# Linear attention into a routed expert layer: float32 key-value sums, a planned engine order, regrouped transfers

## The chip, the cores and the metric

One core of a Trainium2 chip runs the whole program in one launch. The metric is the device time in microseconds (us) of one execution, as a median of several runs. A core has five engines with instruction queues of their own: PE (TensorE, matrix products; the loads of its weights are listed apart as PEld), DVE (VectorE), ACT (ScalarE), POOL (GpSimd) and SP (SyncE, which here only issues DMA transfers). TensorE's clock is granted at one of two levels, 1.2 or 2.4 GHz; a "granted clock" of 1.00 in a row means 2.4 GHz throughout the stretch.

## The reference, cut to what matters

```python
q, k, v: [8 batches, 8 heads, 576, 64]; w_phi: [64, 128]
def phi(x):
    proj = x @ w_phi
    proj = proj - max(abs(proj), axis=-1)
    return concat([exp(proj), exp(-proj)])     # 256 features
kv  = phi(k).T @ v          # per batch and head: [256, 64]
z   = sum(phi(k), over the 576 positions)
att = (phi(q) @ kv) / (phi(q) @ z + 1e-6)      # -> x [4608, 512]
x = (((x @ w1) * (x @ w2)) @ w3) @ w_out       # [4608, 512]
e = argmax(x @ w_gate); g = softmax(x @ w_gate)[e]
out = g * (relu(x @ e_w1[e]) @ e_w2[e])        # 8 experts
```

All inputs and outputs are float32.

## The kernel before, in words

Nearly every product is made of three float16 matmuls: each operand is split into a high part and a low part (the value less the high part), and high*high, high*low and low*high are summed in PSUM.

**First part.** The eight batches go in four units of two. In a unit, `group` (line 469) handles two heads at a time, four groups to a unit, 16 groups in all. Keys and queries are loaded (`load`), split (`split`), transposed by DMA (`trans`) and multiplied by w_phi (`proj`, lines 547 and 548), each in three chunks of 128x384. On the key side, per head and chunk: `k_max` and `k_sub` take off the row maximum, `k_exp` (line 575) makes exp(-x) in float32 and, through `exp16` (lines 554 and 556), exp(x) twice, as float16 and float32; `exp_lo` (line 561) makes the low part of exp(x) on DVE. `k_s1` to `k_s3` find, once all three chunks of a head have their maxima, a power of two that scales exp(-x); `k_c1` (ACT, line 604) and `k_c2` (DVE, line 609) split the scaled exp(-x). Values are scaled to a power of two from the sum of their squares (`v_norm`, `v_sum`, `v_scale`) and split by `v_hi` (ACT, line 532) and `v_lo` (DVE, line 540). `k_b` (line 612) then sums phi(k).T @ [v, 1]: for each of ten pieces of a head and each sign it issues three float16 matmuls of 65 columns (line 626), 60 a head, 1920 for 32 of them (two heads of each of 16 groups, both batches of the unit together). `kv_hi` (line 633) and `kv_lo` (line 638) split the sum for the queries, whose side (`q_max` to `q_x`) ends in the 65-column matmuls of line 702 and in `xn`.

After a unit's four groups, `x_prep` and `moe1` (lines 757 and 793) do the dense products: lines 806 to 808 (128x384) and line 843 (128x260); then the routing, and each token's row goes to `rows_d` in DRAM. The next unit's attention runs beside it. In the background `w34_setup` and `moe_weight` convert the dense weights (lines 214 to 218, 404, 411), and `expert_weight` (line 289) does the 16 expert matrices: one load of 2 MB into the single buffer `wf`, squares, a scale, then eight pieces that are split (lines 321 and 325) and stored to `wscr` in DRAM, 256 KB each, through four buffers `pc`.

**Second part.** `phase_b` (line 1155) runs 40 slots of 128 tokens of one expert (lines 1127 to 1129 and 1146 to 1148) with expert weights read from `wscr` by transfers of 4 MB. It lies under `manual_schedule`, as written.

**What sets the order.** Every step is filed by hand with a due time, `at(t, fn)`, offsets in the table `O`; the sorted list is the order in which the program is written. From it the framework lays out each engine's queue in the first part: it picks, by run times of its own, among instructions that it takes to be ready, the earlier written first. On the chip each engine then follows its queue strictly.

Of the kernel before, what the change touches and what calls it, by code (L numbers as in the profile page):

```python
# [8 lines left out]
F32 = mybir.dt.float32  # L9
# [15 lines left out]
NE = 8  # L25
# [11 lines left out]
    k_s1=2.37, k_s2=3.06, k_s3=3.08, k_c1=3.31, k_c2=3.4, k_b=3.51, kv_hi=5.55, kv_lo=5.74,  # L37
# [23 lines left out]
E23 = float(2 ** 23)  # L61


@with_exitstack
def kernel(
# [23 lines left out]
        [NE, P, 2, 2, 4096], F16, name="wscr")  # L89
# [199 lines left out]
    def expert_weight(e, idx, t0):  # L289
        src = (e_w1, e_w2)[idx][e]  # L290
        nk = (4, 8)[idx]
        st = {}

        def load():
            st["wf"] = pools["prep"].tile([P, 4096], F32, tag="wf", name="wf")
            nc.sync.dma_start(st["wf"].rearrange("p (k f) -> p k f", k=nk),
                              src.rearrange("(k p) f -> p k f", p=P))
            st["cm"] = stat.tile([P, 4], F32, tag="ecm", name="ecm")

        def square(j):  # L300
            sq = pools["mp"].tile([P, 2 * DM], BF16, tag="junk", name="junk")
            A.activation(sq, st["wf"][:, j * 1024:(j + 1) * 1024], AF.Square, accum_out=st["cm"][:, j:j + 1])

        def scale0():
            st["cs"] = stat.tile([P, 1], F32, tag="ecs", name="ecs")
            V.tensor_reduce(st["cs"], st["cm"], axis=AX.X, op=ALU.add)

        def scale1():
            st["pn"] = psum.tile([P, 512], F32, tag="ts", bufs=1, name="pe")
            T.matmul(st["pn"][:, 0:1], lhsT=ones32, rhs=st["cs"], start=True, stop=True)  # L310

        def scale2():
            st["s"], si = pow2_scale(st["pn"][:, 0:1], 1, CE[idx], "es")
            if idx == 0:
                V.tensor_copy(fexp[:, e:e + 1], si)
            else:
                V.tensor_tensor(fexp[:, e:e + 1], fexp[:, e:e + 1], si, op=ALU.mult)

        def piece_hi(j):
            st["pc", j] = pools["prep"].tile([P, 2, 512], F16, tag="pc", bufs=4, name="pc")  # L320
# [9 lines left out]
        for j in range(4):  # L330
            at(t0 + O["e_sq"] + O["e_sq_j"] * j, square, j)
# [14 lines left out]
    def w34_setup(t0, dt, t1):  # L346
# [4 lines left out]
        def start():  # L351
            st["wo"] = pools["prep"].tile([P, 8, DM], F32, tag="wf", name="wo")
            wg = su.tile([P, 4, NE], F32, name="wg")
            nc.sync.dma_start(wg, w_gate.rearrange("(k p) e -> p k e", p=P))
            st["wg"] = wg
            st["wog"] = su.tile([P, 8, NE], F32, name="wog")
            for i in range(3):
                f = pools["prep"].tile([P, 2, 512], F16, tag="pc", bufs=4, name="f34")
                st["f34", i] = f.rearrange("p a c -> p (a c)").bitcast(F32)
            st["fg"] = const.tile([P, 8, NE], F32, name="fg")  # L360
# [108 lines left out]
    def group(ui, g, T0):  # L469
# [33 lines left out]
        def v_load(h):  # L503
            vf = att.tile([P, 10, D], F32, tag="vf", bufs=2, name="vf")
            G.memset(vf[64:128, 4, :], 0.0)
            G.memset(vf[0:64, 9, :], 0.0)
            for bb, b in enumerate(bs):
                nc.sync.dma_start(vf[:, 5 * bb:5 * bb + 4, :],
                                  v[b, h0 + h, 0:512, :].rearrange("(p r) d -> p r d", r=4))
                nc.sync.dma_start(vf[64 * bb:64 * bb + 64, 9 if bb else 4, :], v[b, h0 + h, 512:S, :])  # L510
            st["vf", h] = vf

        def v_norm(h):
            vs = att.tile([P, 10, 2, D + 1], F16, tag="vs", bufs=2, name="vs")
            st["ssv", h] = stat.tile([P, 1], F32, tag="ssv", name="ssv")
            A.activation(vs[:, :, 0, 0:D], st["vf", h], AF.Square, accum_out=st["ssv", h])
            st["vs", h] = vs
# [11 lines left out]

        def v_hi(h):  # L530
            vs = st["vs", h]
            A.activation(vs[:, :, 0, 0:D], st["vf", h], AF.Copy, scale=st["sv", h][:, 0:1])
            G.memset(vs[:, :, 0, D:D + 1], ZS)
            G.memset(vs[:, :, 1, D:D + 1], 0.0)
            G.memset(vs[64:128, 4, 0, D:D + 1], 0.0)
            G.memset(vs[0:64, 9, 0, D:D + 1], 0.0)

        def v_lo(h):
            vs = st["vs", h]
            V.scalar_tensor_tensor(vs[:, :, 1, 0:D], st["vf", h], st["sv", h][:, 0:1], vs[:, :, 0, 0:D],  # L540
                                   op0=ALU.mult, op1=ALU.subtract)
# [60 lines left out]
        def k_c1(h, c):  # L602
            hl = att.tile([P, 2, 3, P], F16, tag="k2", bufs=2, name="k2")
            A.activation(hl[:, 0], st["ke2", h, c], AF.Copy, scale=st["fk"][:, h:h + 1])
            st["k2", h, c] = hl

        def k_c2(h, c):
            hl = st["k2", h, c]
            V.scalar_tensor_tensor(hl[:, 1], st["ke2", h, c], st["fk"][:, h:h + 1], hl[:, 0],
                                   op0=ALU.mult, op1=ALU.subtract)  # L610

        def k_b(h, c):
# [4 lines left out]
            kv, vs = st["kv"], st["vs", h]  # L617
            for t in range(3):
                tt = 3 * c + t
                for bb, p0, _ in tile_parts(tt):  # L620
                    tv = 9 if p0 else tt
                    end = tt == 8 or (tt == 4 and bb == 0)
                    for z in range(2):
                        hl = st["k2", h, c] if z else st["k1", h, c][0]
                        for a, b in ((0, 0), (0, 1), (1, 0)):
                            T.matmul(kv[:, bb, z, :], lhsT=hl[:, a, t, :], rhs=vs[:, tv, b, :],
                                     start=False, stop=bool(end and a), skip_group_check=True)

        def kv_hi(h):
            if h == 0:  # L630
                st["kvs"] = att.tile([P, 2, 2, 2, 2, D + 1], F16, tag="kvs", bufs=1, name="kvs")
            for z in range(2):
                A.activation(st["kvs"][:, 0, h, z], st["kv"][:, :, z, :], AF.Copy, scale=2.0 ** -10 if z else 1.0)

        def kv_lo(h):
            ks = st["kvs"]
            for z in range(2):
                V.scalar_tensor_tensor(ks[:, 1, h, z], st["kv"][:, :, z, :], 2.0 ** -10 if z else 1.0, ks[:, 0, h, z],
                                       op0=ALU.mult, op1=ALU.subtract)
# [366 lines left out]
    def load_w(ln, e, cond=None):  # L1006
        kw = dict(cond=cond, cond_hint=False) if cond is not None else {}
        src = wscr[e] if isinstance(e, int) else wscr[bass.ds(e, 1)].rearrange("o p a b f -> (o p) a b f")
        nc.sync.dma_start(wb[ln], src, **kw)

    def open_b():
        right.close()
        pools["wb"] = tc_pool(wb_st, "wb", "right")
        wb[0] = pools["wb"].tile([P, 2, 2, 4096], F16, name="wb0")
        wb[2] = pools["wb"].tile([P, 2, 2, 4096], F16, name="wb2")
# [100 lines left out]
    def slot_l1(n):  # L1116
# [3 lines left out]
        for mh in range(2):  # L1120
            ph = psum.tile([P, 4, P], F32, tag="mm", bufs=3, name="ph")
            for mm in range(4):
                m = 4 * mh + mm
                for kk in range(4):
                    wh = w[:, 0, 0, kk * FF + m * P:kk * FF + (m + 1) * P]
                    wl = w[:, 0, 1, kk * FF + m * P:kk * FF + (m + 1) * P]
# [9 lines left out]
    def slot_l2(n, hT):  # L1136
# [6 lines left out]
        for i2 in range(8):  # L1143
            wh = w[:, 1, 0, i2 * DM:(i2 + 1) * DM]
            wl = w[:, 1, 1, i2 * DM:(i2 + 1) * DM]
# [9 lines left out]
    def phase_b():  # L1155
# [4 lines left out]
        wb[1] = B2["pb"].tile([P, 2, 2, 4096], F16, name="wb1")  # L1160
# [4 lines left out]
        V.tensor_copy(wb[1][:, 0, 0, 0:1], xq[1][:, 0, 0, 0:1])  # L1165
# [29 lines left out]
    at(t_end + 1, phase_bm)  # L1195

# [33 lines left out]
```

## Time and profile before

| | us |
|---|---|
| median of 3 runs | 1639.8 (1636.98 to 1642.35) |
| profiled execution | 1653.94 |
| its span, first to last instruction | 1652.2 |
| mean granted clock of TensorE over the span | 0.936 |
| PE busy | 1428.4 (86%) |
| DVE busy | 1001.4 (61%) |
| ACT busy | 881.7 (53%) |

Busy times count instructions between start and end; ends of matmuls are modelled, and consecutive ones overlap, so a busy PE may have room, and the pace of matmuls is read from their starts. "Idle" before a group is time in which its engine waited just before it, and "<-" names what ended that wait.

### The profile page before, as it was taken

Reading aid. Unit: us, or ns where it says so; the run is one execution under the profiler, and the core shown is the slowest. Engines: PE = TensorE matmul, PEld = TensorE weight load, DVE = VectorE, ACT = ScalarE, POOL = GpSimd, SP = SyncE. Lnnn points to the kernel's source line nnn. Section 1 sums busy time; section 2 is a strip of 40 time slices with the busy share of each in tenths; the row PEclk is TensorE's granted clock in tenths of the full one; section 3 lists DMA queues with packets and bytes.
Section 4 is the critical chain, followed back from the end, with each engine's and each line's share of the span. In section 5 each row is a group of like instructions: output and inputs, shape, how many; then the busy total and the mean of one; then the engine's idle time right before and its main releaser. Section 6 shows DMA issues by size and latency. Waiting matters only on the chain. (4 is left out here: it accounts for less than half of the span.)

```text
span 1652.2 us, 38216 instructions
## 1 busy us (share of the span) xinstructions
PE 1428.4 (86%) x14850; PEld 1032.2 (62%) x14854; DVE 1001.4 (61%) x3031; ACT 881.7 (53%) x1979; POOL 226.9 (14%) x491
## 2 busy tenths in 40 slices
PE   5988877888898796889697998968949999999998
PEld 4665555666665474657475766636746777777775
DVE  6998899987898696879697898434411111111111
ACT  4786688777786685768576777335201111111111
POOL 3313100010111010100101000100102111121110
PEclk9988777998999798999898999979979999999999
DMA  7845245575767775574955665963346346747351
GB/s 200 237 125 157 73 124 100 153 124 126 134 170 124 123 166 66 159 146 115 149 159 97 161 101 139 188 191 116 51 145 193 76 83 172 250 104 178 78 170 31
DMA packets 273043, 225.16 MB, mean 136 GB/s; under 512 B 187221, under 2 KB 244825, under 8 KB 271706
## 3 DMA queue, kind: packets, MB, share of 16 engines
q1 hardware_dynamic: 265306, 202.71, 53.5%
q0 software_dynamic: 7552, 19.97, 4.2%
q8 instruction: 118, 1.93, 0.6%
q14 instruction: 67, 0.55, 0.2%
HBM read 261.22 MB, written 53.67 MB: 191 GB/s over the span
## 5 line engine op out<-in xcount | busy, mean ns | idle before, releaser
L806 PE MATMUL pab<-xT,w 128*128 128x384 f16 x768 | 258.8, 337 | 26.1 <-ACT asb L813 16.1
L1132 DVE SCALAR_TENSOR_TENSOR hT<-ph,hT 128x512 f16<-128x512 f32 x80 | 55.3, 692 | 362.6 <-ACT hT L1131 362.6
L807 PE MATMUL pab<-xT,w 128*128 128x384 f16 x768 | 258.8, 337 | 0.0
L808 PE MATMUL pab<-xT,w 128*128 128x384 f16 x768 | 258.3, 336 | 0.0
L1127 PE MATMUL ph<-xTb,wb 128*128 128x128 f16 x1280 | 218.4, 220 | 22.6 <-DMA xTb<-rw 22.6
L843 PE MATMUL py<-w,gt 128*128 128x260 f16 (+1 forms) x1728 | 213.6, 278 | 16.5 <-ACT yb L850 12.1
L1128 PE MATMUL ph<-xTb,wb 128*128 128x128 f16 x1280 | 218.3, 220 | 0.0
L1129 PE MATMUL ph<-xTb,wb 128*128 128x128 f16 x1280 | 218.3, 220 | 0.0
L843 PEld LDWEIGHTS <-gt 128*128 128x128 f16 x1728 | 166.6, 100 | 43.3 <-issue 13.3
L1131 ACT ACTIVATE hT<-ph 128x512 f16<-128x512 f32 x80 | 47.8, 597 | 187.5 <-PE ph L1129 187.5
L1127 PEld LDWEIGHTS <-wb 128*128 128x128 f16 x1280 | 125.9, 98 | 27.9 <-DMA xTb<-rw 21.1
L1128 PEld LDWEIGHTS <-wb 128*128 128x128 f16 x1280 | 125.9, 98 | 4.5
L1129 PEld LDWEIGHTS <-wb 128*128 128x128 f16 x1280 | 125.9, 98 | 0.0
L1150 ACT ACTIVATE ob<-pob,scb 128x512 f32<-128x512 f32 x40 | 27.5, 687 | 183.4 <-PE pob L1148 183.4
L554 ACT ACTIVATE q<-pjT,nM 128x384 f16<-128x384 f32 x192 | 114.9, 598 | 17.2 <-PE nm L702 14.1
L702 PE MATMUL nm<-kvs,q 128*128 128x65 f16 (+1 forms) x1920 | 86.7, 201 | 41.3 <-DVE nx L712 37.4
L1146 PE MATMUL pob<-wb,hT 128*128 128x512 f16 x320 | 121.3, 379 | 0.0
L1147 PE MATMUL pob<-wb,hT 128*128 128x512 f16 x320 | 121.3, 379 | 0.0
L1148 PE MATMUL pob<-wb,hT 128*128 128x512 f16 x320 | 121.3, 379 | 0.0
L321 ACT ACTIVATE pc<-wf,ess 128x512 f16<-128x512 f32 x128 | 88.8, 726 | 57.2 <-DMA wscr<-pc 50.1
L556 ACT ACTIVATE e<-pjT,nM 128x384 f32<-128x384 f32 x192 | 116.0, 604 | 5.8 <-DVE q L561 5.8
L702 PEld LDWEIGHTS <-q 128*128 128x128 f16 (+1 forms) x1920 | 76.9, 104 | 66.1 <-issue 38.0
(255 smaller groups left out, 3237.5 us busy)
## 6 DMA issues: line engine op xcount, KB each, us to landing
wb<-wscr SPq DMA_DIRECT2D x40, 4096.0 KB
wf<-in_moe_w_dram SPq DMA_DIRECT2D x16, 2048.0 KB
wscr<-pc SPq DMA_DIRECT2D x128, 256.0 KB
raw<-in_moe_w_dram SPq DMA_DIRECT2D x32, 512.0 KB
rows_d<-row SPq DMA_DIRECT2D x32, 256.5 KB
kf<-in_k_dram SPq DMA_DIRECT2D x64, 128.0 KB
vf<-in_v_dram SPq DMA_DIRECT2D x64, 128.0 KB
qf<-in_q_dram SPq DMA_DIRECT2D x64, 128.0 KB
```

Of the source, the lines that this page charges most:

```text
L556: A.activation(e1, src, AF.Exp, scale=sgn * ES, bias=bias)
L702: T.matmul(nm[p0:p1, t, z, :], lhsT=hl[:, a, t, p0:p1], rhs=st["kvs"][:, b, h, z, bb, :], start=(a == b), stop=bool(a), skip_group_check=True)
L806: T.matmul(ps, lhsT=wh, rhs=xT[:, 0, kk], start=(kk == 0), stop=False)
L807: T.matmul(ps, lhsT=wh, rhs=xT[:, 1, kk], start=False, stop=False)
L808: T.matmul(ps, lhsT=wl, rhs=xT[:, 0, kk], start=False, stop=(kk == 3))
L843: T.matmul(py, lhsT=gT[i][:, a, t * P:(t + 1) * P], rhs=w34[:, i, b, hf, 0:cw], start=(i == 0 and a == b), stop=bool(i == 7 and a))
L1127: T.matmul(ph[:, mm, :], lhsT=wh, rhs=xT[:, 0, kk, :], start=(kk == 0), stop=False)
L1128: T.matmul(ph[:, mm, :], lhsT=wh, rhs=xT[:, 1, kk, :], start=False, stop=False)
L1129: T.matmul(ph[:, mm, :], lhsT=wl, rhs=xT[:, 0, kk, :], start=False, stop=(kk == 3))
L1146: T.matmul(po, lhsT=hT[:, 0, i2, :], rhs=wh, start=(i2 == 0), stop=False)
L1147: T.matmul(po, lhsT=hT[:, 0, i2, :], rhs=wl, start=False, stop=False)
L1148: T.matmul(po, lhsT=hT[:, 1, i2, :], rhs=wh, start=False, stop=(i2 == 7))
```

## The change

Three things are edited in the first part; the second part's arithmetic is unchanged.

1. `k_b` multiplies float32 exponentials with float32 values, one matmul in place of three. exp(x) and exp(-x) are made once each; the splits of both and of v go. The scales that these splits carried are applied in `kv_hi` and `kv_lo`, for the 64 sums and for the count column apart, with three small DVE instructions a head (`kv_s`) to make them. The count column of ones lies in `vf`, whose rows are 65 wide now.
2. Just before the second part is written, `plan` reads all instructions written so far, gives each a duration (in the diff in ns: `hold`, for which it occupies its engine, and `time`, until its result is there), simulates the engines with their dependencies and buffers (each engine takes, among those ready, the earliest written) and chains each engine's instructions in the resulting order.
3. Transfers: the two heads' loads of keys or queries become one transfer; each 2 MB load of expert weights becomes four of 512 KB, due 0.4 apart; the 128 stores of split pieces become 64 of 512 KB (two pieces in one of two buffers). `wscr` is laid out so that such a store is one run of 4 KB in a partition; the second part indexes it accordingly.

```diff
+class Step:
...
+        if self.dma:
+            if self.engine == "Pool":
+                self.hold, self.time = 1250, 10000
+            elif kind == "DmaTransposeAnt":
+                self.hold, self.queue, self.time = 1300, 1250, 2000
+            else:
+                self.hold, self.queue, self.time = 480, 100 + b / 280, 2000
+        elif kind == "Matmult":
+            n *= 4 if inns[0].dtype == F32 else 1
+            self.hold = max(28, n / 2.4 + 2) * 1.0
+            self.time = self.hold + 170
...
+        else:
+            if self.engine == "DVE":
+                t = 145 + n * (1.1 if two or psum or kind == "TensorReduce" else 0.6)
+            elif self.engine == "Pool":
+                t = 150 + n * (2.2 if two else 1.2)
+            else:
+                t = 200 + 0.93 * n
...
+            self.hold, self.time = max(62, t - OVERLAP[self.engine]), t
...
+def plan(tc, insts, follows):
...
+    for _ in steps:
+        t, e = min((max(free[e], 0.0 if takes[e] else waits[e][0][0]), e) for e in engines if takes[e] or waits[e])
+        while waits[e] and waits[e][0][0] <= t:
+            heapq.heappush(takes[e], heapq.heappop(waits[e])[1])
+        n = heapq.heappop(takes[e])
...
+        if e in prev:
+            tc.add_manual_dep(s.ins, prev[e].ins.name, info, reason="planned order")
+        prev[e] = s
...
-            nc.sync.dma_start(st["wf"].rearrange("p (k f) -> p k f", k=nk),
-                              src.rearrange("(k p) f -> p k f", p=P))
+        def load_part(j):
+            k0, kn = j * nk // 4, nk // 4
+            nc.sync.dma_start(st["wf"].rearrange("p (k f) -> p k f", k=nk)[:, k0:k0 + kn, :],
+                              src[k0 * P:(k0 + kn) * P, :].rearrange("(k p) f -> p k f", p=P))
...
-            nc.sync.dma_start(wscr[e, :, idx, :, j * 512:(j + 1) * 512], pc)
+            if j % 2:
+                nc.sync.dma_start(wscr[e, :, idx, j - 1:j + 1], st["pp", j // 2])
...
-                for h in range(2):
-                    nc.sync.dma_start(
-                        t[:, h, 5 * bb:5 * bb + 4, :],
-                        src[b, h0 + h, 0:512, :].rearrange("(p r) d -> p r d", r=4))
+                nc.sync.dma_start(
+                    t[:, :, 5 * bb:5 * bb + 4, :].rearrange("p h r d -> p h (r d)"),
+                    src[b, h0:h0 + 2, 0:512, :].rearrange("h (p r) d -> p h (r d)", r=4))
...
-            vf = att.tile([P, 10, D], F32, tag="vf", bufs=2, name="vf")
+            vf = att.tile([P, 10, D + 1], F32, tag="vf", bufs=2, name="vf")
+            G.memset(vf[:, :, D:D + 1], 1.0)
...
         def k_exp(h, c):
-            e2 = att.tile([P, 3, P], F32, tag="ke2", bufs=3, name="ke2")
-            A.activation(e2, pm, AF.Exp, scale=-ES)
-            exp16(("k1", h, c), pm, 1.0, "k1", 3)
-            st["ke2", h, c] = e2
+            for z in range(2):
+                e = att.tile([P, 3, P], F32, tag="ke%d" % (z + 1), bufs=3, name="ke%d" % (z + 1))
+                A.activation(e, pm, AF.Exp, scale=-ES if z else ES)
+                st["ke", z, h, c] = e
...
                     for z in range(2):
-                        hl = st["k2", h, c] if z else st["k1", h, c][0]
-                        for a, b in ((0, 0), (0, 1), (1, 0)):
-                            T.matmul(kv[:, bb, z, :], lhsT=hl[:, a, t, :], rhs=vs[:, tv, b, :],
-                                     start=False, stop=bool(end and a), skip_group_check=True)
+                        T.matmul(kv[:, bb, z, :], lhsT=st["ke", z, h, c][:, t, :], rhs=vf[:, tv, :],
+                                 start=False, stop=bool(end), skip_group_check=True)
...
+        def kv_s(h):
+            ks = stat.tile([P, 3], F32, tag="kss", bufs=3, name="kss")
+            fk, sv = st["fk"][:, h:h + 1], st["sv", h]
+            V.tensor_scalar(ks[:, 0:1], fk, 2.0 ** -10, None, op0=ALU.mult)
+            V.tensor_tensor(ks[:, 1:2], ks[:, 0:1], sv, op=ALU.mult)
+            V.tensor_scalar(ks[:, 2:3], fk, ZS * 2.0 ** -10, None, op0=ALU.mult)
...
+                for (c0, c1), sc in zip(((0, D), (D, D + 1)), st["kss", h][z]):
+                    A.activation(st["kvs"][:, 0, h, z, :, c0:c1], st["kv"][:, :, z, c0:c1], AF.Copy, scale=sc)
...
-            for fn in (v_load, v_norm, v_sum, v_scale, v_hi, v_lo, k_s1, k_s2, k_s3, kv_hi, kv_lo):
+            for fn in (v_load, v_norm, v_sum, v_scale, k_s1, k_s2, k_s3, kv_s, kv_hi, kv_lo):
...
-                for fn in (k_max, k_sub, k_exp, k_c1, k_c2, k_b):
+                for fn in (k_max, k_sub, k_exp, k_b):
-                at(tk + O["k_lo"], exp_lo, ("k1", h, c))
...
+    def plan_a():
+        body = max(nc.cur_f.blocks, key=lambda b: len(b.instructions))
+        plan(tc, list(body.instructions), (("su", "mp"), ("att", "wb"), ("att", "tb")))
+    at(t_end + 0.99, plan_a)
```

## Rows read from the trace of the kernel before

**Rows 1.** The chain that ended last, first piece: start us, us, what.

```profile
1627.97 0.98 DMA out_dram<-ob,ix
```

**Rows 2.** Windows by stage: us, busy PE, PEld, DVE, ACT, POOL, PEclk, DMA, GB/s.

```profile
0.00:36.00 36.00, 18.82 (x91) 17.18 (x91) 19.93 (x46) 14.09 (x28) 10.96 (x48) 1.00 0.74 202
36.00:1030.00 994.00, 837.06 (x8855) 602.98 (x8860) 845.20 (x2605) 727.55 (x1695) 120.95 (x343) 0.91 0.62 135
1030.00:1220.00 190.00, 148.57 (x1106) 101.85 (x1104) 78.11 (x262) 64.84 (x138) 18.14 (x22) 0.91 0.56 128
1220.00:1652.00 432.00, 423.92 (x4800) 310.18 (x4800) 58.18 (x121) 75.25 (x120) 76.88 (x78) 0.99 0.51 138
```

**Rows 3.** The same view in stretches of 50 us, four of the attention stage.

```profile
400.00:450.00 50.00, 45.61 (x534) 34.91 (x532) 42.97 (x143) 39.81 (x94) 7.18 (x23) 1.00 0.63 138
...
500.00:550.00 50.00, 36.13 (x303) 23.67 (x302) 36.32 (x123) 26.60 (x66) 4.45 (x13) 0.83 0.84 114
...
600.00:650.00 50.00, 34.17 (x368) 23.50 (x365) 31.99 (x115) 28.72 (x68) 6.96 (x19) 0.86 0.74 102
650.00:700.00 50.00, 45.76 (x531) 34.94 (x530) 43.60 (x139) 38.78 (x92) 4.66 (x20) 1.00 0.56 157
```

**Rows 4.** Waits: who <- for whom: us in total, times, longest.

```profile
ACT pc L321 <- DMA wscr<-pc: 50.1, 13, 17.9
...
ACT junk L302 <- DMA wf<-in_moe_w_dram: 35.9, 10, 11.8
...
DVE sp L491 <- DMA qf<-in_q_dram: 23.3, 4, 16.6
PE ph L1127 <- DMA xTb<-rw: 22.6, 2, 20.9
```

**Rows 5.** Groups by form: DVE instructions that the change removes.

```profile
L609 DVE SCALAR_TENSOR_TENSOR k<-ke,fk,k 128x384 f16<-128x384 f32 x96 | 59.7, 623 | 1.7 <-ACT k L604 1.7
...
L561 DVE TENSOR_TENSOR k<-e,k 128x384 f16<-128x384 f32 x96 | 54.0, 562 | 22.9 <-ACT e L556 20.6 <-ACT k L554 2.0
...
L540 DVE SCALAR_TENSOR_TENSOR vs<-vf,vss,vs 128x640 f16<-128x640 f32 x32 | 28.6, 892 | 0.3 <-ACT vs L532 0.2
```

**Rows 6.** Groups by form: ACT instructions that the change removes.

```profile
L604 ACT ACTIVATE k<-ke,fk 128x384 f16<-128x384 f32 x96 | 56.4, 607 | 18.5 <-DVE fk L599 9.6 <-PE kv L626 8.2 <-DVE w L274 0.6
...
L554 ACT ACTIVATE k<-pm 128x384 f16<-128x384 f32 x96 | 50.1, 522 | 5.3 <-PE kv L626 5.3
...
L532 ACT ACTIVATE vs<-vf,vss 128x640 f16<-128x640 f32 x32 | 26.8, 838 | 2.7 <-DVE vss L194 2.3 <-DVE vsi L196 0.4
```

**Rows 7.** Groups by form: small instructions on DVE and ACT.

```profile
L721 DVE TENSOR_TENSOR rec<-rec,svi 128x6 f32<-128x6 f32 x48 | 7.6, 158 | 0.1
...
L586 ACT ACTIVATE rk<-mk 128x9 f32<-128x9 f32 x32 | 6.9, 216 | 4.7 <-DVE mk L566 4.7
```

**Rows 8.** Timeline of PE, three stretches: start us, us to the last end, instruction, count.

```profile
63.35 1.85 PE L411 MATMUL pg<-wog,w3t 128*128 128x8 f32 x16
65.06 0.27 PE L615 MATMUL kv<-zero 128*128 128x260 f16 x1
...
71.98 1.88 PE L404 MATMUL p<-wo,w3t 128*128 128x512 f32 x4
73.69 0.60 PE L396 MATMUL pt<-ident,w 128*128 128x128 f32 x4
...
680.22 0.90 PE L626 MATMUL kv<-vs,k 128*128 128x65 f16 x24
680.96 0.27 PE L843 MATMUL py<-w,gt 128*128 128x260 f16 x1
```

**Rows 9.** DMA queue of SP: packets, MB, share of 16 engines; two issue groups.

```profile
q1 hardware_dynamic: 265306, 202.71, 53.5%
...
wf<-in_moe_w_dram SPq DMA_DIRECT2D x16, 2048.0 KB
...
vf<-in_v_dram SPq DMA_DIRECT2D x64, 128.0 KB
```

More of the change, by code (lines that the diff above doesn't have):

```diff
@@ L1 @@
+import heapq
+from collections import defaultdict
 from contextlib import ExitStack
@@ L36 @@
     k_load=-4.63, k_split=-2.6, k_trans=-2.5, k_proj=0.05, k_max=0.3, k_sub=0.41, k_exp=0.52, k_lo=0.75,
-    k_s1=2.37, k_s2=3.06, k_s3=3.08, k_c1=3.31, k_c2=3.4, k_b=3.51, kv_hi=5.55, kv_lo=5.74,
+    k_s1=2.37, k_s2=3.06, k_s3=3.08, k_c1=3.31, k_c2=3.4, k_b=3.51, kv_s=3.2, kv_hi=5.55, kv_lo=5.74,
     v_load=-0.7, v_norm=0.3, v_sum=1.05, v_scale=1.55, v_hi=1.7, v_lo=2.54,
@@ L61, with sizes, __init__, cells @@
 E23 = float(2 ** 23)
+BYTES = {F32: 4, I32: 4, F16: 2, BF16: 2, U8: 1}
+OVERLAP = dict(DVE=80, Activation=105, Pool=-25)
+WAKE = 60
+LANES = 8
+SPARE = 0
+DMA_SPARE = 0
+def sizes(ap):
+    n, span = 1, 1
+    for step, count in ap.ap[1:]:
+        n *= count
+        span += (count - 1) * abs(step)
+    return n, span
+class Step:
+    def __init__(self, ins):
+        self.ins, self.engine = ins, str(ins.engine).rsplit(".", 1)[-1]
+        kind = type(ins).__name__.removeprefix("Inst")
+        self.dma = "DMA" in kind.upper()
+        outs = [a for a in ins.outs if hasattr(a, "bass_ap")]
+        inns = [a for a in ins.ins if hasattr(a, "bass_ap")]
+        self.reads, self.writes = [self.cells(a) for a in inns], [self.cells(a) for a in outs]
+        n = max(sizes(a)[0] for a in (outs if kind != "TensorReduce" else inns)) if outs else 1
+        psum = any(c[0] == "P" for c in self.reads)
+        two = sum(sizes(a)[0] > 1 for a in inns) > 1
+        self.queue = 0.0
+        if self.dma:
+            b = n * 128 * BYTES.get(outs[0].dtype, 4)
+            if self.engine == "Pool":
[8 more added lines that the diff above has]
+            self.time = self.hold + 170
+            self.spare = SPARE if sizes(outs[0])[0] < 20 else 0
+        else:
[5 more added lines that the diff above has]
+                t = 200 + 0.93 * n
+            if len(outs) > 1:
+                t += 190
+            self.hold, self.time = max(62, t - OVERLAP[self.engine]), t
+        self.after, self.begins, self.left, self.ready, self.start = [], [], 0, 0.0, 0.0
+    @staticmethod
+    def cells(a):
+        ap = a.bass_ap
+        t = ap.tensor
+        where = str(getattr(t, "space", "DRAM")).rsplit(".", 1)[-1][0]
+        if not hasattr(t, "tag"):
+            return ("D", t.name, None, ())
+        if where != "S":
+            return (where, t.name, t, (0,))
+        b = BYTES.get(a.dtype, 4)
+        row = t.bytes() // 128
+        lo = ap.offset * b % row
+        p0 = ap.offset * b // row
+        hi = lo + sizes(a)[1] * b
+        halves = [h for h, on in ((0, p0 < 64), (1, p0 + ap.ap[0][1] > 64)) if on]
+        return ("S", t.name, t, tuple((k, h) for k in range(lo // 32, (hi - 1) // 32 + 1) for h in halves))
@@ new lines, in plan, with arm @@
+def plan(tc, insts, follows):
+    steps = [Step(i) for i in insts if i.outs and "PoolBoundary" not in type(i).__name__]
+    last, readers, users, uses_pool = {}, defaultdict(list), defaultdict(list), defaultdict(list)
+    order = defaultdict(list)
+    for n, s in enumerate(steps):
+        for _, name, t, _ in s.reads + s.writes:
+            if t is not None:
+                if not users[name]:
+                    order[t.tag].append((name, t.tag_meta.bufs))
+                    pool = t.tag.rsplit("_", 2)[1]
+                    uses_pool[pool].append(name)
+                if users[name][-1:] != [n]:
+                    users[name].append(n)
+    deps, begun = [set() for _ in steps], [set() for _ in steps]
+    for n, s in enumerate(steps):
+        for acc, wr in ((s.reads, False), (s.writes, True)):
+            for w, name, t, cells in acc:
+                for c in cells:
+                    k = (name, c)
+                    if k in last:
+                        deps[n].add(last[k])
+                    if wr:
+                        deps[n].update(readers[k])
+                    elif w == "P":
+                        for m in readers[k][-1:]:
+                            (begun if steps[m].engine == s.engine else deps)[n].add(m)
+        for w, name, t, cells in s.reads:
+            for c in cells:
+                readers[name, c].append(n)
+        for w, name, t, cells in s.writes:
+            for c in cells:
+                last[name, c], readers[name, c] = n, []
+    for n, s in enumerate(steps):
+        if s.dma and s.engine == "SP":
+            for d in [d for d in deps[n] if steps[d].dma and steps[d].engine == "SP"
+                      and {w[1] for w in steps[d].writes} & {w[1] for w in s.writes}]:
+                deps[n].discard(d)
+                begun[n].add(d)
+    for tag, tiles in order.items():
+        for j, (name, bufs) in enumerate(tiles):
+            if j:
+                for n in users[name]:
+                    begun[n].add(users[tiles[j - 1][0]][0])
+            if j >= bufs:
+                old = users[tiles[j - bufs][0]]
+                for n in users[name]:
+                    deps[n].update(old)
+    for a, b in follows:
+        old = [n for name in uses_pool[a] for n in users[name]]
+        for name in uses_pool[b]:
+            for n in users[name]:
+                deps[n].update(old)
+    for n, s in enumerate(steps):
+        deps[n].discard(n)
+        begun[n].discard(n)
+        s.left = len(deps[n]) + len(begun[n])
+        for d in deps[n]:
+            steps[d].after.append(n)
+        for d in begun[n]:
+            steps[d].begins.append(n)
+    free, waits, takes = defaultdict(float), defaultdict(list), defaultdict(list)
+    lanes, queue = [0.0] * LANES, 0.0
+    for n, s in enumerate(steps):
+        if not s.left:
+            heapq.heappush(waits[s.engine], (0.0, n))
+    engines = sorted({s.engine for s in steps})
+    prev = {}
+    info = mybir.DependencyInfo(mybir.DependencyClass.NoSync, mybir.DependencyReason.DATA)
+    def arm(m, r):
+        o = steps[m]
+        o.ready = max(o.ready, r)
+        o.left -= 1
+        if not o.left:
+            heapq.heappush(waits[o.engine], (o.ready, m))
+    for _ in steps:
[3 more added lines that the diff above has]
+        n = heapq.heappop(takes[e])
+        s = steps[n]
+        if s.dma and e == "SP":
+            t = max(t, lanes[0])
+            queue = max(queue, t + s.hold) + s.queue
+            end = queue + s.time
+            lanes = lanes[1:] + [end]
+        else:
+            end = t + s.time
+        s.start, free[e] = t, t + s.hold
+        for m in s.after:
+            o = steps[m]
+            if o.engine != e or s.dma:
+                arm(m, end + WAKE + (o.spare if o.engine == "PE" else 0) + (DMA_SPARE if s.dma and o.engine != "SP" else 0))
+            else:
+                arm(m, t if e == "PE" else end + 35)
+        for m in s.begins:
+            arm(m, t)
+        if e in prev:
+            tc.add_manual_dep(s.ins, prev[e].ins.name, info, reason="planned order")
+        prev[e] = s
+    return steps
@@ L528, in v_scale @@
             st["sv", h] = s
[L530 to L541, printed above, removed]
         def proj(nm, h, c):
@@ L637, in kv_lo @@
             for z in range(2):
-                V.scalar_tensor_tensor(ks[:, 1, h, z], st["kv"][:, :, z, :], 2.0 ** -10 if z else 1.0, ks[:, 0, h, z],
-                                       op0=ALU.mult, op1=ALU.subtract)
+                for (c0, c1), sc in zip(((0, D), (D, D + 1)), st["kss", h][z]):
+                    V.scalar_tensor_tensor(ks[:, 1, h, z, :, c0:c1], st["kv"][:, :, z, c0:c1], sc,
+                                           ks[:, 0, h, z, :, c0:c1], op0=ALU.mult, op1=ALU.subtract)
         def q_max(c, h):
```

52 lines of the change are left out of this document (24 added, 28 removed).

## The prediction

> **What bounds the kernel now.** The chain of waits comes first and helps little: it starts at 1628 us [rows 1] and holds only the last outputs. So I read the windows by stage, then the same view finer, then the waits. The stages [rows 2] are a start of 36 us; the attention stage to 1030, with dense products and conversions beside it; a tail of 190, the last unit's dense products; and the second part, 432, where PE is busy for 424 and which the change only indexes differently. The attention stage has no single bound. Of its 994 us PE is busy 837, DVE 845, ACT 728, and TensorE's clock is granted at 0.91 of 2.4 GHz. The finer windows [rows 3] show two kinds. In some, the clock is 1.00 and PE is busy 45.6 or 45.8 of 50, with DVE at 43 to 44. In others PE and DVE both drop to 32 to 36, with the DMA share up to 0.84. The waits [rows 4] say that transfers are part of these dips: ACT waits 50.1 us for stores of expert pieces and 35.9 for the 2 MB loads, DVE 23.3 for query loads, once for 16.6. PE, DVE and ACT lie close together, so taking work off one of them is worth little unless the order fills the others.
>
> The profiled execution took 1653.9 us, 1.7 outside its span. The median of the runs is 1639.8, so I make the sum on the profiled execution and multiply by 1639.8/1653.9 = 0.9915.
>
> **Part 1, float32 sums.**
> DVE loses three groups [rows 5]: 59.7 + 54.0 + 28.6 = 142.3 us. It gains 64 one-column instructions in kv_lo and 3 x 32 in kv_s, 160 at the 158 ns of a 128x6 instruction [rows 7], 25 us. Net -117.
> ACT loses 56.4 + 50.1 + 26.8 = 133.3 us [rows 6] and gains 64 small instructions in kv_hi at 216 ns [rows 7], 14 us. Net -119.
> PE: before, 24 matmuls of line 626 take 0.74 us from the first start to the next group's start [rows 8], 31 ns each; 1920 take 59 us. After, there are 640 float32 matmuls of 65 columns. The trace has no such shape. A float32 matmul in the code leaves two records, and there are two neighbours [rows 8]. At 8 columns, 16 records take 1.71 us, 107 ns each. At 512 columns, 4 records take 1.71 us, 428 ns each, so columns cost 0.84 ns and 65 would cost 54. Since 8 columns can't fill 107 ns, that is the weight load, and it hides under long column streams but not under 54 ns. Lower end: only columns, 2 x 54 = 108 ns, 69 us. Upper end: load and columns in turn, 2 x 161 = 322 ns, 206 us. I take 2 x 107 = 214 ns, 137 us, nearest to the 8-column row. Net +78, from +10 to +147. The planner itself prices such a matmul at 260/2.4 + 2 = 110 ns, so it fills about 66 us of PE time twice over.
> Beside this, the Trainium skill, "FP8 and Floating Point Precision", section "TensorE Precision Notes", counts true FP32 as four passes through the array. The 512-column row agrees, but by passes alone 65 columns come to an estimated 108 ns and the sum to +10 instead of +78; the 8-column row stands against that.
> Waits: k_b now needs only k_exp and the values, no longer the scale found from all three chunks, so a chain of ACT, PE and DVE leaves its path. In exchange vf is held until the head's last k_b where it was free after v_lo. Behind a late vf stand, on SP's queue, the key loads and transposes, and DVE and PE wait for those. There are two buffers and v_load is due 2.8 steps of the due times (9 make a group) after the k_b that frees its buffer, so I charge nothing.
>
> **Part 3, transfers.** A 2 MB load no longer keeps the queue for itself; this can return part of the 35.9 and 23.3. Pieces are stored in pairs through two buffers, so ACT may wait longer for each; I leave the 50.1 between 0 and 100 at its value. SP issues 64 fewer key and query loads, 64 fewer stores, 48 more expert loads. Against it, a row of vf of 65 values cuts the 64 large value loads [rows 9] from 1 KB runs to 256 B, 512 for 128 packets each: 24,600 more. At the queue's mean, 53.5% of 1652 us x 16 over 265,306 packets = 53 ns, that is 82 us on each of 16 engines, against as many packets fewer in the stores, whose bytes remain. Bounds: nothing, and 0.08 more of DMA share in 994 us. Cover is the prefetch of values; I charge nothing and keep it in the range.
>
> **Part 2, the order, and the sum.** PE becomes the busiest engine of the attention stage: 837 at 0.91 clock is 762 at full clock, plus 78 is 840. DVE comes to 728, ACT to 609. What counts is how full PE is, times its clock, over the stage: now 762/994 = 0.77. With 840 the stage breaks even at 0.845. The windows without dips reach 0.91 at clock 1.00 [rows 3], with DVE at 0.87, more than it will then need (728/920 = 0.79). I expect the plan with less DVE and ACT work to hold that mean: 840/0.913 = 920, -74 us. In the tail, 190 less 149 busy is 41 idle, of which 21 is the wait for the first rows of the second part [rows 4], which no edit touches; I take half of the other 20, -10. The start and the second part: 0. Sum -84: 1653.9 - 84 = 1570, times 0.9915 = **1557 us**.
>
> **Rivals.**
> *PE binds at its present fill* (slower). The added 78 us sit on an engine that stalls as before, since plan and chip differ by 104 ns on each of 640 matmuls and a fixed order can't give way. At 0.77, 840/0.77 = 1091, +97: 1736. For it: the dips are transfers' and the bytes stay. Against: DVE and ACT, for which PE waits, lose 14% and 16%. It decides below 0.845. Chance 0.12.
> *The order gives nothing* (no change). The framework already fills the queues by times of its own; only the trade remains, PE lands at about 0.845, and 1640 stays. For it: windows at 0.91 exist already. Against: they alternate with windows at 0.68 to 0.72. Chance 0.11.
> *DVE stays the bound* (faster still). If PE's extra work all falls into its 157 idle us, the stage goes with DVE at its present fill: 728/0.85 = 856, -138, with the tail -148: 1493. For it: with 845 of 994 us it is the busiest of the three now, and what it loses is the largest single saving. Against: PE would have to be 840/856 = 0.98 full. Chance 0.12.
>
> **How the numbers follow.** The forecast has 0.65, within itself 1505 to 1610 (fill 0.96 to 0.88 with the same tail: 840/0.96 = 875 gives 1512; 840/0.88 = 955 gives 1591; the rest is the price of the float32 matmul). The range 1490 to 1640 takes in the DVE case, the no-change case and both ends of PE's price at the forecast's fill (+10 gives 1483, +147 gives 1632, nearly all of it inside), and leaves out the slow rival and a little below. A measurement of this kernel can tell about 0.3% from no change. Faster by more: the forecast, the DVE case and half of no change, 0.82; same 0.04; slower 0.14.
>
> **What would show it.** Right: L561 for k, L609, L540, L604 and L532 gone; twice 640 float32 records at 107 ns start to start; the attention stage near 920 us with PE above 0.9 in most 50 us windows, clock near 1.00, DVE near 0.8; waits for wf and qf shorter; tail and second part within 10 us. Wrong: float32 records at 54 or 161 ns; dips with high DMA share that remain; PE waiting on DMA for Tkf, or SP on PE for vf; PE fill times clock under 0.845.

## The result and the profile after

The change takes 1614.4 us (1611.4 to 1618.0) against 1640.4 for the kernel before: ratio 0.984, interval 0.981 to 0.987; in a later comparison 0.986 (0.982 to 0.990). It is faster, by 26 us where 83 were forecast. The profiled executions differ by 36 us in span (1652.2 and 1616.1); the one of before lay 0.9% over its median, the one after 0.2%, so some 10 of these 36 us belong to the two executions and not to the change.

The page of the kernel after, part 1, engine TensorE:

```profile
PE 1488.6 (92%) x14212; PEld 1125.3 (70%) x14214; DVE 908.2 (56%) x2967; ACT 789.1 (49%) x1819; POOL 201.5 (12%) x395
```

PE is 60 us busier and DVE and ACT are each 93 us less busy. The windows by stage, after (columns as in [rows 2], which they answer):

```profile
0.00:36.00 36.00, 23.08 (x113) 21.74 (x113) 18.09 (x36) 13.52 (x26) 11.70 (x44) 1.00 0.82 236
36.00:1000.00 964.00, 893.45 (x8195) 691.34 (x8197) 755.17 (x2565) 636.21 (x1539) 97.45 (x252) 0.94 0.66 137
1000.00:1190.00 190.00, 153.66 (x1170) 107.53 (x1169) 76.96 (x247) 64.69 (x136) 15.33 (x21) 0.91 0.55 135
1190.00:1616.00 426.00, 418.44 (x4741) 304.71 (x4738) 57.97 (x120) 74.66 (x119) 77.05 (x78) 1.00 0.52 137
```

The attention stage went from 994 to 964 us, where 920 were forecast. The tail's windows are 190 us wide by choice of their ends; its length is read from single lines below. PE's work in the stage, 893 at a clock of 0.94, is 840 us at full clock, the forecast's 840 (within some 4 us, as the clock has two digits). What is short is how full the stage is: 840/964 = 0.87, not 0.91.

Cut at the first unit's end, before and after (windows, same columns; before first):

```profile
36.00:260.00 224.00, 183.99 (x1723) 129.33 (x1727) 201.99 (x550) 170.94 (x392) 46.01 (x100) 0.84 0.52 140
260.00:1000.00 740.00, 627.15 (x6849) 453.08 (x6849) 618.78 (x1977) 535.30 (x1250) 73.89 (x240) 0.94 0.65 133
```

```profile
36.00:260.00 224.00, 201.29 (x1577) 154.23 (x1578) 179.35 (x545) 146.76 (x350) 35.97 (x74) 0.87 0.53 135
260.00:1000.00 740.00, 692.15 (x6620) 537.11 (x6620) 575.82 (x2022) 489.45 (x1190) 61.48 (x178) 0.96 0.69 138
```

After, PE busy times clock is 0.78 of the first unit and 0.90 of the rest. The first unit's end and the start of the second part are read from the first start of lines 806 and 1127, by the view of single lines (instruction, count, least/median/greatest ns, first and last start); the end of the whole attention stage is read from the last start of line 702, the queries' last products. Before:

```profile
L702 PE MATMUL nm<-kvs,q x1920: 190/194/263, 76.1 to 1022.9; 128*128 128x65 f16 x160, 128*64 128x65 f16 x32
...
L806 PE MATMUL pab<-xT,w x768: 322/326/528, 265.1 to 1181.6; 128*128 128x384 f16 x192
...
L1127 PE MATMUL ph<-xTb,wb x1280: 216/219/314, 1220.9 to 1641.1; 128*128 128x128 f16 x183
```

After, the same three lines of the program:

```profile
L878 PE MATMUL nm<-kvs,q x1920: 190/194/263, 77.1 to 991.7; 128*128 128x65 f16 x160, 128*64 128x65 f16 x32
...
L981 PE MATMUL pab<-xT,w x768: 322/326/528, 263.3 to 1144.9; 128*128 128x384 f16 x192
...
L1303 PE MATMUL ph<-xTb,wb x1280: 216/219/314, 1184.5 to 1604.9; 128*128 128x128 f16 x183
```

The first unit ends 2 us sooner and the attention stage 31; from there to the second part it is 193 us in place of 198, so the tail is 5 us shorter. The second part begins 36 us sooner and then takes as long as before. So nearly the whole gain lies in the units after the first.

### The profile page after: what moved, and what is told of

Same layout as the page of the kernel before. It is cut to its first block, busy times and chain, and to the rows that moved or that the text cites. A ratio compares the mean times of both kernels' runs of the same rounds, so it can differ in the third digit from the quotient of the medians.

```text
span 1616.1 us, 36510 instructions
## 1 busy us (share of the span) xinstructions
PE 1488.6 (92%) x14212; PEld 1125.3 (70%) x14214; DVE 908.2 (56%) x2967; ACT 789.1 (49%) x1819; POOL 201.5 (12%) x395
## 5 line engine op out<-in xcount | busy, mean ns | idle before, releaser
L1018 PE MATMUL py<-w,gt 128*128 128x260 f16 (+1 forms) x1728 | 206.0, 274 | 0.0
L791 PEld LDWEIGHTS kv<-vf,ke 128*128 128x128 f32 x1280 | 172.9, 211 | 12.2 <-issue 7.4
L791 PE MATMUL kv<-vf,ke 128*128 128x65 f32 x1280 | 176.3, 291 | 3.8 <-issue 2.1
L738 DVE TENSOR_TENSOR q<-e,q 128x384 f16<-128x384 f32 x192 | 108.0, 565 | 36.9 <-ACT e L733 35.8
L982 PEld LDWEIGHTS <-w 128*128 128x128 f16 x768 | 78.4, 102 | 57.5 <-issue 19.4
```

Source lines behind the costliest of these rows:

```text
L791: T.matmul(kv[:, bb, z, :], lhsT=st["ke", z, h, c][:, t, :], rhs=vf[:, tv, :], start=False, stop=bool(end), skip_group_check=True)
L982: T.matmul(ps, lhsT=wh, rhs=xT[:, 1, kk], start=False, stop=False)
L1018: T.matmul(py, lhsT=gT[i][:, a, t * P:(t + 1) * P], rhs=w34[:, i, b, hf, 0:cw], start=(i == 0 and a == b), stop=bool(i == 7 and a))
```

## The experiments

All ratios are to the kernel before on the same chip, with 95% intervals.

### Which part of the change brings the gain

The three parts of the diff were applied in other combinations: the order alone, the sums alone, the sums with the transfers, the order with the transfers, and the order with the sums. In each the hunks of the other parts are left out, so their lines are those of the kernel before.

```diff
 (order alone; order with the float32 sums, old transfers; order with new transfers, float16 sums)
+    at(t_end + 0.99, plan_a)
 (sums alone; sums with new transfers)
...
+                        T.matmul(kv[:, bb, z, :], lhsT=st["ke", z, h, c][:, t, :], rhs=vf[:, tv, :],
+                                 start=False, stop=bool(end), skip_group_check=True)
```

Expected of the order alone:

> Only the planned order is added; float16 sums and old transfers stay. Theory A (PE is the bound of the attention stage, the order raises its fill, the float32 sums put 78 us of weight loading back on it): most of the gain is here, 1590 to 1620, PE at 0.85 or more of the stage with DVE near 0.9. Theory B (the framework's order was as good; the gain came from the DVE and ACT work removed): 1640 within 5. Theory C (the plan's prices do not hold and its fixed order loses): above 1650.

Of the sums alone:

> Only the float32 sums; the framework's order and old transfers stay. Theory A: PE gets 78 us more in a stage that it fills to 0.84, DVE and ACT lose 117 and 119: between 1630 and 1680. Theory B: 1615, all of the gain. Theory C: below 1615.

Of the sums with the transfers:

> The change without the planned order. Theory A: 1630 to 1670, so the order is worth 20 to 55 us on top of the other two. Theory B: 1615, the order is worth nothing. Theory C: below 1610, the order costs.

Of the order with the transfers:

> The change without the float32 sums: planned order and new transfers with the three float16 matmuls. Theory A: the float32 sums are what keeps the stage long, so this is faster than the whole change, 1570 to 1605. Theory B: 1640. If DVE becomes the bound instead (845 us of work in the stage), the same as the whole change, 1610 to 1620.

Of the order with the sums:

> Planned order and float32 sums with the old transfers. If the regrouped transfers are worth what the waits of the kernel before suggest: 5 to 15 us slower than the whole change, ratio 0.988 to 0.994. If the planned order had already gone around them, or the smaller runs of the values cost it back: 0.982 to 0.988.

Of the change itself, beside later kernels:

> The changed kernel itself, beside the next three and the kernel before on one chip: ratio to before 0.984 as in the first comparison, which places the runs of the planned order with float16 sums (0.988) within 0.005 of it.

| order | sums | transfers | ratio | interval |
|---|---|---|---|---|
| framework | float32 | old | 0.998 | 0.996 to 1.001 |
| framework | float32 | new | 0.9995 | 0.997 to 1.002 |
| planned | float16 | old | 0.990 | 0.987 to 0.993 |
| planned | float16 | new | 0.988 | 0.983 to 0.993 |
| planned | float32 | old | 0.993 | 0.991 to 0.996 |
| planned | float32 | new | 0.984, 0.986 | 0.981 to 0.990 |

The gain is the order's: 1.0% alone, about 1.5% on top of the other two. It isn't one lucky order, for every planned kernel here and below that does the whole arithmetic lies at 0.968 to 0.993. Theory B falls: without the order, sums and transfers are worth nothing measurable. Theory A is right on the order and wrong on the sums: they neither keep the stage long nor shorten it, with or without the order. The order with float16 sums came out as the whole change does, as was expected if DVE becomes the bound there; DVE is busy for 854 us of the same window, against 755 after the change (windows of that kernel):

```profile
36.00:1000.00 964.00, 836.22 (x8894) 611.31 (x8895) 853.87 (x2638) 734.07 (x1706) 118.62 (x351) 0.92 0.64 139
```

So the float32 sums may be an even trade of DVE's time for PE's; no run tests that. New transfers gain about 0.8% under the planned order with float32 sums; in the other two pairs they stay within the intervals. They also give another order, and a nudge of the plan moves a kernel as much (below), so the 0.8% isn't shown to be theirs. The waits of [rows 4] on transfers became shorter (kernel after, waits):

```profile
ACT pc L509 <- DMA wscr<-pc: 21.2, 7, 6.5
...
ACT junk L488 <- DMA wf<-in_moe_w_dram: 10.2, 4, 8.6
DVE sp L681 <- DMA qf<-in_q_dram: 9.6, 2, 5.2
```

With the old transfers under the same order and sums (waits of that kernel) the first two stand at

```profile
ACT pc L504 <- DMA wscr<-pc: 22.5, 7, 9.9
...
ACT junk L485 <- DMA wf<-in_moe_w_dram: 14.9, 4, 7.4
```

so most of the shortening of these two is there without the new transfers.

### Is it PE that paces the stage?

Three kernels take work away, each from the changed kernel. Fewer sums:

```diff
                     for z in range(2):
+                        if tt not in (0, 4, 8):
+                            continue
                         T.matmul(kv[:, bb, z, :], lhsT=st["ke", z, h, c][:, t, :], rhs=vf[:, tv, :],
```

> Leaves out 12 of the 20 float32 sums of a head (only three of nine position tiles are summed), 384 of 640 matmuls, 82 us of PE at 214 ns; nothing is taken from DVE or ACT. Theory A: at fill times clock of 0.87 the first part ends 90 us sooner, total about 1520 to 1540. Theory D: PE is only busy beside the waits, 10 to 35 us sooner. If half: PE paces some units and not others.

Less setup (the gate's products in the same way):

```diff
-                T.matmul(p34, lhsT=st["w3t", i][:, j, :], rhs=st["wo"][:, j, :], start=(j == 0), stop=(j == 7))
+                if j == 0:
+                    T.matmul(p34, lhsT=st["w3t", i][:, j, :], rhs=st["wo"][:, j, :], start=True, stop=True)
```

> Leaves out seven eighths of the float32 products that prepare the combined dense weights (w3 times w_out and times the gate), 60 us of PE work, all in the first unit. Theory A: the first unit, where fill times clock is 0.80, ends 60 to 75 us sooner. Theory D: 0 to 15 us sooner, since the unit is paced by the attention chain or by the conversions, which stay.

No conversion:

```diff
-        xi = dst.bitcast(I32)
-        V.scalar_tensor_tensor(z, xi, 3, z, op0=ALU.logical_shift_left, op1=ALU.bitwise_or)
-        V.scalar_tensor_tensor(xi, xi, -2 ** 31, z, op0=ALU.bitwise_and, op1=ALU.bitwise_or)
```

> The changed kernel without the two DVE instructions of each of 40 conversions of the dense weights (these weights then have no meaning), 55 us of DVE work in the first unit. If DVE with its conversions paces the first unit: its attention ends 45 to 60 us before the 255 to 260 of the changed kernel. If the order around the float32 sums does (theory E): at most 20 us before. The total may be longer, as the routing is another; the first unit's end tells.

The routing differs in all three and the second part runs three slots more (1376 matmuls in place of 1280), so the totals, 0.982, 1.016 and 0.996, say nothing; the starts do (the second part began at 1184.5 after the change). Fewer sums, the two lines as above:

```profile
L983 PE MATMUL pab<-xT,w x768: 322/326/528, 248.1 to 1091.3; 128*128 128x384 f16 x192
...
L1305 PE MATMUL ph<-xTb,wb x1376: 216/219/314, 1131.9 to 1601.3; 128*128 128x128 f16 x197
```

Less setup, line and window of the first unit:

```profile
L982 PE MATMUL pab<-xT,w x768: 322/326/528, 265.1 to 1145.5; 128*128 128x384 f16 x192
```

```profile
36.00:260.00 224.00, 176.33 (x1361) 148.15 (x1362) 181.16 (x549) 146.98 (x352) 35.05 (x74) 0.70 0.52 135
```

No conversion, the same two views, with the second part's line:

```profile
L978 PE MATMUL pab<-xT,w x768: 322/326/528, 249.9 to 1109.9; 128*128 128x384 f16 x192
...
L1300 PE MATMUL ph<-xTb,wb x1376: 216/219/314, 1148.3 to 1614.4; 128*128 128x128 f16 x197
```

```profile
36.00:260.00 224.00, 208.89 (x1611) 159.81 (x1615) 153.87 (x514) 157.41 (x381) 31.92 (x76) 0.85 0.58 142
```

With 60 us of PE work gone from the first unit, it ends at 265 as before (263). That doesn't show that the time is not PE's, for the clock fell from 0.87 to 0.70 and the matmuls that were left took longer: the float32 sums 369 ns on average in place of 320, and ACT waited twice as long for them. Groups by form from 36 to 260 us and waits from 36 to 262, after the change and with less setup:

```profile
L791 PE MATMUL kv<-vf,ke 128*128 128x65 f32 x331 | 53.3, 320 | 1.6 <-ACT ke L756 1.6
...
ACT kvs L808 <- PE kv L791: 11.6, 5, 6.7
```

```profile
L792 PE MATMUL kv<-vf,ke 128*128 128x65 f32 x339 | 67.0, 369 | 0.7 <-ACT ke L757 0.6
...
ACT kvs L809 <- PE kv L792: 23.1, 7, 6.7
```

The lower clock may have taken back what the missing work gave; no run separates the two. With 55 us of DVE work gone the first unit ends at 250, 13 sooner, and the second part begins 36 sooner. With a quarter of the 82 us of sums gone (20 us) the first unit ends at 248, 15 sooner. In the units after the first, the other 62 us of sums are worth 37 (52.6 in all, 1184.5 to 1131.9, less 15.2).

Each of these kernels also has an order planned anew, and a nudge of the plan alone moves the first unit's end by 14 us (248 to 262, below). So 13 and 15 us in that unit say little, while 52.6 and 36 us at the start of the second part are beyond the 13 us that the nudge moves a whole kernel: the sums on PE and the conversions on DVE both cost time. Neither theory holds for the whole stage: the sums pace the later units in good part, and the setup work taken off PE in the first unit is not given back as time. That the first unit is paced by how the queues wait on one another is a reading, not shown.

### What the plan's prices do

If waits between queues pace, the order is what matters, and the plan prices the sums at 110 ns where the trace has 216. True price for every float32 matmul:

```diff
-            self.hold = max(28, n / 2.4 + 2) * 1.0
+            self.hold = max(28, n / 2.4 + 2, 214 if inns[0].dtype == F32 else 0) * 1.0
```

> Only the plan's price of a float32 matmul is changed, to at least 214 ns (two records of 107 ns in the trace) from 110. Theory A (PE with its clock paces the attention stage, and the order mis-times 66 us of it): faster than the whole change by 10 to 25 us. Theory D (the stage is paced by waits that the plan's prices do not touch): within 6 us of the whole change.

The factor 1.05, then 1.1, in place of 1.0 at the end of that line:

> True float32 price and every matmul 5% longer in the plan, nearer to a granted clock of 0.95. Theory E: 0.972 to 0.979, near the true price or a little better. Theory F: anywhere from 0.970 to 0.990.

> True float32 price and every matmul 10% longer in the plan. Theory G (the plan takes PE for quicker than it is on the chip, so its queues hand PE work too late or too densely; each step towards the chip's PE time gains): 0.958 to 0.970. Theory F (each new order scatters): 0.972 to 0.990.

The factor 1.05 on the old line:

> The changed kernel with every matmul 5% longer in the plan and the old 110 ns for the sums (115 with the 5%). Theory G: between the change (0.985) and both corrections (0.968), 0.973 to 0.982. If the float32 price is what matters: 0.983 to 0.988. Theory F: anywhere.

The price on the sums alone (`... and sizes(outs[0])[0] == 65`):

> Only the 640 float32 sums are priced at 214 ns; one-column and setup float32 matmuls keep the old price. Theory E: 0.972 to 0.978, the whole gain of the true price. If the one-column matmuls, whose results scale the keys and values, carry it (the float16 sums gained from the same price too): 0.981 to 0.988.

The true price, then the true price with the factor 1.05, on the kernel with planned order, new transfers and float16 sums:

> Planned order with the true float32 price, new transfers, but the three float16 matmuls for the sums. Theory E (the 110 ns price spoiled the order around the 640 float32 sums): nothing to spoil here, so ratio 0.985 to 0.991 as with the old price (0.988), and slower than the float32 sums at the true price (0.9755) by 12 to 25 us. Theory F (any new order scatters by that much, the price was luck): anywhere from 0.972 to 0.995.

> Float16 sums, new transfers, and the plan's prices of the run at 0.968. Theory G: the order gains here too, 0.968 to 0.977, so that the float32 sums are worth at most 10 us. Theory E (the price spoiled the order around the float32 sums alone): 0.976 to 0.984.

Last, `WAKE = 65` in place of 60, on the change and on the kernel with the sums' price:

> The changed kernel, the plan's delay between engines at 65 ns in place of 60: another order with the same wrong price. Theory E (the price of the sums is the cause): 0.981 to 0.989, as the change (0.984, 0.986). Theory F (orders scatter by a per cent): as likely below 0.978 as above.

> The same nudge with the 640 sums priced at 214 ns. Theory E: 0.966 to 0.977, as without the nudge (0.971), and below the run beside it by 0.008 to 0.018. Theory F: no such order between the two.

| plan's price of a float32 matmul | other edit | float32 sums | float16 sums |
|---|---|---|---|
| old (110 ns) | none | 0.984, 0.986 | 0.988 |
| old | WAKE 65 | 0.985 (0.982 to 0.989) | |
| old | all matmuls +5% | 0.982 (0.979 to 0.986) | |
| 214 ns, sums alone | none | 0.971 (0.966 to 0.975) | |
| 214 ns, sums alone | WAKE 65 | 0.979 (0.975 to 0.983) | |
| 214 ns, all | none | 0.976 (0.972 to 0.979) | 0.978 (0.976 to 0.981) |
| 214 ns, all | all matmuls +5% | **0.968** (0.965 to 0.971) | 0.974 (0.971 to 0.977) |
| 214 ns, all | all matmuls +10% | 0.991 (0.988 to 0.994) | |

Five pairs of kernels differ in the price alone: none, none with the sums alone, WAKE 65, +5%, and the float16 sums. In each the true price is faster, by 0.7% to 1.4% (11 to 23 us). Theory A of this section had forecast 10 to 25 us for the first, and it gave about 15. Against it stands the +10%: it has the true price and no partner at the old one, lies at 0.991, and if it is counted the float32 kernels of the two prices overlap and their means differ by 0.7% in place of 1.1%. Scatter is real: the nudge moves one kernel by nothing and the other by 0.8%, and its pair came out at the edge of what theory E allowed (0.979 against at most 0.977, 0.007 apart against at least 0.008). So single steps of this size between orders prove nothing; the sign over five pairs speaks for the price, and how much it is worth isn't told from the scatter. Theory G falls: with 10% more the gain is gone. The float16 kernel gained from the true price as well, which theory E excluded; there only setup and one-column float32 matmuls change price. Which of their instructions it is stays open.

In the fastest of all, 1583.6 us (3.2% under the kernel before), the first unit and the rest of the stage look like this (windows):

```profile
36.00:260.00 224.00, 204.57 (x1710) 153.84 (x1713) 205.60 (x629) 167.49 (x400) 39.78 (x77) 0.94 0.60 148
260.00:1000.00 740.00, 692.40 (x6614) 532.47 (x6614) 571.08 (x1975) 482.18 (x1162) 61.22 (x179) 0.97 0.62 140
```

```profile
L981 PE MATMUL pab<-xT,w x768: 322/326/528, 240.8 to 1105.8; 128*128 128x384 f16 x192
...
L1303 PE MATMUL ph<-xTb,wb x1280: 218/219/311, 1143.4 to 1563.8; 128*128 128x128 f16 x183
```

The first unit ends at 241 in place of 263, with DVE at 0.92 of the window (206 of 224) in place of 0.80, and the second part begins 41 us sooner than after the change (the medians differ by 31). Up to its first dense product, PE busy times clock is 0.86 (185 x 0.95 of 204), where the first unit had 0.78 after the change, with the same work to do:

```profile
36.00:240.00 204.00, 185.15 (x1592) 141.86 (x1594) 187.01 (x562) 151.50 (x359) 39.78 (x77) 0.95 0.61 153
```

Of the float32 kernels of the table, those with the old price ended the first unit at 259 to 264, those with the true one at 241 to 248, all but one. The first unit isn't all of it, though. With the sums' price alone, without and with the nudge, it ended at 248 and 262, and the latter still took 0.979:

```profile
L981 PE MATMUL pab<-xT,w x768: 322/326/528, 248.0 to 1123.0; 128*128 128x384 f16 x192
```

```profile
L981 PE MATMUL pab<-xT,w x768: 322/326/528, 262.2 to 1141.2; 128*128 128x384 f16 x192
```

And the kernel with +10% ended its first unit at 243 and lost the time again later: its second part began at 1184, as after the change.

## Why the prediction was right and wrong

**Right: the direction, the trade and its prices.** The order brings the gain that there is, the sums trade DVE and ACT work for PE work, and the stage's PE work came out at 840 us as summed. A timeline of PE in the kernel after shows the float32 price:

```profile
321.70 1.90 PE L791 MATMUL kv<-vf,ke 128*128 128x65 f32 x16
323.43 0.83 PE L1018 MATMUL py<-w,gt 128*128 128x260 f16 x6
```

16 records in 1.73 us are 108 ns each, 216 a matmul, where 107 and 214 were taken from the 8-column row [rows 8]. The count of four passes in the Trainium skill, "FP8 and Floating Point Precision", section "TensorE Precision Notes", gave an estimated 108 ns a matmul; the trace shows twice that, so here the measurement decides. The pace is the same at 8 and at 65 columns, so columns don't set it; that the load of the weights does is the prediction's reading, which no run tests alone.

**Nearly right: DVE and ACT.** On the page both fell by 93 us, not by 117 and 119. The prediction had added up instructions one by one, though, and summed so, over all groups by form, DVE fell by 107 (1206.9 to 1099.5) and ACT by 122 (1048.9 to 927.2). The 10 that DVE lacks are mostly kv_lo, 34.0 us now against 16.0 (groups of the kernel after):

```profile
L814 DVE SCALAR_TENSOR_TENSOR kvs<-kv,vss,kvs 128x128 f16<-128x128 f32 x32 | 11.1, 346 | 0.9 <-ACT kvs L808 0.9
L814 DVE SCALAR_TENSOR_TENSOR kvs<-kv,kss,kvs 128x128 f16<-128x128 f32 x32 | 11.0, 343 | 0.0
L814 DVE SCALAR_TENSOR_TENSOR kvs<-kv,kss,kvs 128x2 f16<-128x2 f32 x32 | 6.9, 217 | 0.0
L814 DVE SCALAR_TENSOR_TENSOR kvs<-kv,kvs 128x2 f16<-128x2 f32 x32 | 5.0, 155 | 0.0
```

I had let the wide half keep 284 ns and added 158 for the narrow one.

**Wrong: the step "I expect the plan with less DVE and ACT work to hold that mean: 840/0.913 = 920, -74 us".** This step failed: less DVE and ACT work did not make the plan hold the fill of the two best windows over the whole stage. It held 0.87, 0.78 in the first unit and 0.90 after it. The 0.913 came from windows [rows 3] in which dense products stand beside the attention; the first unit has none. By that step its 155 us of PE work at full clock (184 x 0.84) plus a quarter of the 78 would have taken 174/0.913 = 191 us, -33; it gave -2. The units after it, near the mean assumed, gave -29 of the remaining -41. The DVE and ACT work, which was to let the fill rise, gave nothing measurable by itself (0.998). Why the first unit stayed at 0.78 is only partly known: the missing dense products aren't the whole of it, since the same work without them reached 0.86 in the fastest kernel, by other prices and so another order. The prediction also read the windows with dips at 0.68 to 0.72; that is PE's busy share alone, and times the clock of [rows 3], as it counts elsewhere, they stand at 0.59 and 0.60.

**Wrong by 5 us: the tail.** Half of its idle time, 10 us, was to go; it became 5 us shorter (198 to 193).

**The slow rival was half right.** It said that plan and chip differ by 104 ns on each of 640 matmuls and that a fixed order can't give way. It put the break-even at 0.845; the stage reached 0.87, so the change is faster. But I had charged this error at nothing in the forecast, and the five pairs put it at 11 to 23 us, with a scatter between orders of up to 13. That is at most two fifths of the 57 us by which the forecast fell short; the rest stays open.

**The wait on vf** is there: SP's queue waits for the sums (waits of SP, kernel after), 58.4 us in 15 waits, each at most 10.1. No run tried a third buffer, so its cost is open.

```profile
SPq L701 <- PE kv L791: 58.4, 15, 10.1
```

## What to carry to other kernels

Before a fill read from good windows is spread over a stage, ask what fills them, and leave out the units that lack it. Where an order is planned ahead, price its instructions by the trace's start-to-start times: here a wrong price went with about 1%, while a tenth or more of their work taken off two engines gave nothing measurable without the new order. And compare several orders before believing a per cent: a nudge of 5 ns in an unrelated constant moved one kernel by 0.8%. The same holds when work is left out to see what it was worth, if the order is planned anew each time.

## What the hardware showed unexpectedly

Taking PE work away lowered the granted clock: with 60 us of it removed from the first unit, PE was busy 176 us in place of 201, the clock fell from 0.87 to 0.70, the matmuls that were left took longer (the sums 369 ns in place of 320), and the unit's end stayed. So leaving out PE's work did not price that work here, as the clock moved with it. Whether the low clock there is only a sign of PE's idle time or a cost of its own isn't shown; the fastest kernel, with the work of the change in another order, had 0.94 there and ended the unit 22 us sooner.
